# Identity transposes put into the start of a fused attention and two-layer kernel, and a loop step in another order

## The chip, the cores and the metric

The kernel runs on one core of a Trainium2 chip. The metric is device time in microseconds (us), the median of the runs. A core has TensorE (PE in the profile; PEld is its weight load), VectorE (DVE), ScalarE (ACT), GpSimd (POOL) and SyncE (SP, which here only issues DMA transfers). Each engine works through its own instructions strictly in order and waits for others through semaphores. [...]

## The reference

Three parts stand one behind the other. `_attn_ref` is attention in chunks of 32 queries, with 16 positions of left and 8 of right context and 8 memory positions, for 4 batches, 8 heads, 768 positions and 64 values a head. `_moe_ref` and `_moe2_ref` are two dense layers over the 3072 tokens.

```python
# attention, per chunk
scores = scale * np.matmul(q_c, k_full.transpose(0, 1, 3, 2))
a = np.exp(scores - np.max(scores, axis=-1, keepdims=True))
a = a / (np.sum(a, axis=-1, keepdims=True) + 1e-09)
out[:, :, c_start:c_end] = np.matmul(a, v_full)
# first layer, 512 -> 1024 -> 512
h = x @ w_in
e = np.exp(h - h_max)
solu = h * (e / (np.sum(e, axis=-1, keepdims=True) + 1e-09))
ln = (solu - mu) / np.sqrt(var + 1e-06) * g_ln
x = ln @ w_out
# second layer, 512 -> 2048 -> 512
h = x @ w_in2
out = (h * np.clip(h + 3.0, 0.0, 6.0) / 6.0) @ w_out2
```

## The kernel before

The 3072 tokens are cut into 24 tiles of 128. The work on a tile goes through short helper functions, each of which issues a few instructions:

- Attention. `q_p` and `k_p` (from tile 10 on `block_p`, 4 transposes for a whole tile) turn queries and keys on TensorE into one of three PSUM tiles `tp` that go round; `q_e`, `k_e`, `block_e` copy them out. `s_p` makes the scores (16 small products into `sc`, 32 matmul records in the trace), `s_max` and `s_sub` (DVE) take the maximum off, `s_exp` (ACT) exponentiates, `s_sum` (DVE) and `s_norm` (POOL in the loop) normalise, `p_p` transposes the probabilities, `p_e` copies them out, `v_p` makes the value products, and `x_h` (ACT) and `x_l` (DVE) split the result into a high and a low part.
- First layer. `m1(i, f)` is half f of the product with `w_in` (12 matmuls, three for each exact product of split numbers). `ln_max` (DVE), `ln_exp` (ACT), `ln_den`, `ln_solu`, `ln_mean` (DVE), `ln_sq` (ACT), `ln_var` (DVE), `ln_pow` (POOL) and `ln_norm` (DVE) make the normalised activation, `ln_t` transposes it (4 transposes a half, then `ln_h` on ACT and `ln_l` on DVE). `m2` makes the product with `w_out` for three tiles together in pieces of 8 matmuls (`piece`), and `m2_e` (DVE) copies a finished block out.
- Weights arrive as 8-byte numbers and are turned into 4-byte ones by `*_abs`, `*_hold` and `*_bits` (two or three DVE operations each).

The order of the instructions is written out by hand. The list `FIRST` gives it for the start (tiles 0 to 8 in part), name by name. From `m = 7` to 23 a loop gives it: step `m` does `m1` and the normalisation of tile m, attention values of tile `a = m + 1`, scores of tile `n = m + 2`, transposes of tile `l = m - 1`, and up to m = 20 the conversion of two pieces of the second layer's weights (`end_w2`). In a step of even m POOL also adds weight blocks (`sum_pair`). `ln_t(m, 0)`, which needs `ln_norm(m)`, comes in the next step, behind `m1(m + 1, 0)`. The second layer (`g3`, `act3`, `split3`, `g4`) follows the loop.

Of the kernel before, what the change touches and what calls it, by code (L numbers as in the profile page):

```python
# [22 lines left out]

STEADY = 7
FIRST = """
    load_q:0 load_w1:3 q_p:0 load_mem_k:0 mem_p:0 mem_e:0,A zero:km0,D zero:v0,D zero:qb,P q_e:0,0,D w1_abs:3,D
# [4 lines left out]
    mem_e:2,A k_e:1,1,A k_e:1,0,A s_exp:0 s_p:1 w1_abs:0,A w1_abs:2,A k_p:2,0 k_e:2,0,A spread_mem_v:0,0,A zero:v1,P
    w1_hold:7,P w1_bits:7,0 w1_bits:1,1 w1_bits:7,1 w1_bits:1,2 w1_bits:7,2 s_sum:0 w1_hold:0,D w1_bits:0,0
    w1_bits:0,1 w1_hi:3,P s_norm:0,D zero:pb,P p_p:0 q_p:2 load_k:3 load_q:3 load_mem_k:1 load_q:4 load_v:1
    p_e:0,0,A p_e:0,1,A spread_mem_v:0,64,A k_p:2,1 v_p:0 w1_bits:0,2 w1_hi:1,D s_max:1 s_sub:1 s_exp:1 q_e:2,0,D
    x_h:0,0 k_e:2,1,D w1_hi:7,A w1_abs:6,A w1_abs:5,A w1_hold:2,P q_e:2,1,D s_p:2 s_sum:1 w1_bits:2,0 w1_bits:2,1
    s_norm:1,D p_p:1 w1_bits:2,2 p_e:1,0,A w1_abs:4,A p_e:1,1,A w1_hi:2,A w1_lo:1,P w1_lo:3,P s_max:2 w1_hold:5,D
    x_l:0,0 w1_hold:4,D w1_bits:5,0 w1_bits:4,0 w1_bits:5,1 load_k:4 load_wo:4 load_g load_v:2 consts w1_hi:0,P
    w1_lo:0,P w1_hold:6,P w1_lo:7,P w1_lo:2,P load_wo:2 m1:0,0,0 early_open k_p:3,1 k_p:3,0 k_e:3,1,A q_p:3
    k_e:3,0,A q_e:3,1,A q_e:3,0,A w1_bits:4,1 s_sub:2 w1_bits:6,0 w1_bits:5,2 mem_p:1 m1:0,0,1 s_p:3 q_p:4
    w1_bits:6,1 w1_bits:4,2 w1_hi:4,D w1_bits:6,2 w1_lo:4,D w1_hi:5,P spread_mem_v:1,0,A s_exp:2 spread_mem_v:1,64,A  # L40
    v_p:1 w1_hi:6,D s_sum:2 s_max:3 s_norm:2,D s_sub:3 q_e:4,1,A x_h:1,0 q_e:4,0,A mem_e:1,A w1_lo:5,P m1:0,1,0
    w1_lo:6,P k_p:4,1 m1:0,1,1 x_l:1,0 k_e:4,1,D p_p:2 k_p:4,0 m1:1,0,0 s_exp:3 ln_max:0 wo_abs:4,A wo_hold:4,D
    s_sum:3 wo_bits:4,0 s_norm:3,P load_wo:0 load_k:5 load_wo:1 p_e:2,0,A k_e:4,0,A s_p:4 m1:1,0,1 ln_exp:0
    p_e:2,1,A v_p:2 wo_abs:2,A wo_bits:4,1 ln_den:0 s_max:4 ln_solu:0 wo_abs:0,D x_h:2,0 wo_hold:0,D wo_bits:4,2
    s_sub:4 x_l:2,0 ln_mean:0 p_p:3 m1:1,1,0 k_p:5,0 m1:1,1,1 m1:2,0,0 k_p:5,1 m1:2,0,1 s_exp:4 k_e:5,0,A ln_sq:0
    p_e:3,0,A p_e:3,1,A wo_bits:0,0 s_sum:4 wo_g:4 wo_hold:2,P wo_bits:0,1 wo_hi:4,D ln_var:0 k_e:5,1,A wo_abs:1,A
    ln_max:1 wo_bits:0,2 ln_exp:1 wo_bits:2,0 ln_pow:0 wo_hold:1,D wo_bits:2,1 s_norm:4,P ln_norm:0 ln_den:1
    load_q:5 load_v:3 load_k:6 m1:2,1,0 q_p:5 v_p:3 q_e:5,1,A q_e:5,0,A x_h:3,1 p_p:4 p_e:4,0,A load_wo:5 load_q:6
    wo_abs:5,A p_e:4,1,A s_p:5 ln_p:0,0 ln_h:0,0,1 k_p:6,1 m1:2,1,1 k_p:6,0 wo_bits:2,2 wo_g:0 ln_solu:1 ln_mean:1
    wo_bits:1,0 wo_bits:1,1 wo_hi:0,D k_e:6,1,A q_p:6 k_mem:6,D ln_sq:1 load_v:4 load_wo:7 v_p:4 load_w2:0 load_q:7  # L50
    load_wo:3 load_k:7 ln_max:2 wo_g:2 s_edge:5 q_e:6,1,A ln_exp:2 ln_var:1 k_e:6,0,D wo_hi:2,D s_max:5 wo_lo:4,P
    x_l:3,1 wo_lo:0,P m1:3,0,0 x_h:4,1 ln_p:0,1 m1:3,0,1 m1:3,1,0 wo_hold:5,P w2_abs:0,A q_e:6,0,A ln_den:2
    wo_lo:2,D wo_bits:1,2 s_sub:5 s_p:6 q_p:7 k_p:7,0 m1:3,1,1 ln_l:0,0,1 x_l:4,1 ln_pow:1 w2_hold:0,P ln_solu:2
    wo_bits:5,0 m1:4,0,0 wo_abs:7,A s_exp:5 ln_h:0,1,1 wo_hold:7,D wo_g:1 s_sum:5 s_norm:5,P s_edge:6 wo_bits:5,1
    ln_mean:2 w2_bits:0,0 k_e:7,0,A wo_abs:3,A wo_hold:3,P ln_l:0,1,1 ln_sq:2 wo_hi:1,A q_e:7,0,A q_e:7,1,A
    ln_norm:1 ln_p:1,0 m1:4,0,1 k_p:7,1 p_p:5 m1:4,1,0 w2_bits:0,1 ln_max:3 ln_exp:3 ln_h:1,0,1 ln_p:1,1 m1:4,1,1
    k_e:7,1,A wo_bits:5,2 wo_lo:1,P load_v:5 load_wo:6 p_e:5,0,A wo_abs:6,D s_max:6 ln_den:3 ln_var:2 ln_pow:2
    ln_l:1,0,1 s_sub:6 s_exp:6 p_e:5,1,A ln_h:1,1,1 ln_l:1,1,1 ln_norm:2 wo_bits:3,0 ln_solu:3 load_k:8 k_p:8,1
    ln_p:2,0 ln_h:2,0,1 ln_l:2,0,1 s_p:7 k_e:8,1,A load_v:6 load_q:8 v_p:5 early_close k_p:8,0 ln_p:2,1 m2:0,0
    wo_bits:3,1 wo_hold:6,D ln_max:4 ln_exp:4 x_h:5,1 k_e:8,0,A s_sum:6 s_norm:6,P x_l:5,1 p_p:6 q_p:8 wo_bits:6,0  # L60
    ln_den:4 ln_mean:3 ln_solu:4 m1:5,0 s_max:7 wo_g:5 wo_bits:3,2 w2_bits:0,2 wo_g:3 wo_hi:5,P wo_lo:5,P
    wo_bits:6,1 wo_hi:3,D m1:5,1 s_sub:7 ln_mean:4 ln_h:2,1,1 ln_l:2,1,1 q_e:8,1,A ln_sq:3 wo_lo:3,D wo_bits:6,2
    m2:0,1 wo_bits:7,0 ln_var:3 wo_g:6 wo_bits:7,1 wo_bits:7,2 wo_g:7 load_k:9 load_w2:1 w2_store:0 load_w2:2
    w2_abs:1,A p_e:6,0,A p_e:6,1,A v_p:6 q_e:8,0,A w2_hold:1,P ln_pow:3 w2_bits:1,0 ln_norm:3 w2_bits:1,1 wo_hi:6,A
    wo_lo:6,P s_exp:7 s_p:8 w2_abs:2,A wo_hi:7,A wo_lo:7,P m2:0,2 m2:0,3 ln_p:3,0 m2:0,4 ln_p:3,1 x_h:6,1 ln_max:5
    w2_bits:1,2 s_sum:7 x_l:6,1 s_norm:7,D p_p:7 m2:0,5 ln_sq:4 ln_exp:5 ln_h:3,0,1 ln_h:3,1,0 ln_den:5 w2_hold:2,P
    ln_solu:5 m1:6,0 w2_bits:2,0 ln_l:3,0,1 s_max:8 m2_e:0,0 m2:0,6 m2:0,7 m1:6,1 load_v:8 load_w2:3 w2_store:1
    w2_abs:3,A w2_hold:3,P w2_bits:3,0 ln_mean:5 p_e:7,1,A ln_sq:5 w2_bits:2,1 p_e:7,0,D ln_var:5 ln_var:4
    w2_bits:3,1 ln_pow:4 ln_pow:5 w2_bits:3,2 ln_l:3,1,0 ln_norm:4 ln_p:4,1 load_v:7 v_p:7 w2_bits:2,2 ln_max:6
    m2_e:0,1 s_sub:8 ln_norm:5 ln_p:4,0 m2:0,8 m2:0,9 ln_exp:6 ln_h:4,1,0 x_h:7,0 ln_den:6 ln_l:4,1,0 ln_p:5,1  # L70
    m2:0,10 ln_solu:6 x_l:7,0 ln_mean:6 ln_p:5,0 m2:0,11 load_w2:5 w2_store:2 w2_store:3 w2_abs:5,A s_exp:8 s_sum:8
    ln_sq:6 ln_var:6 w2_hold:5,P ln_pow:6 s_norm:8,P ln_norm:6 ln_h:5,1,0 load_w2:4 m2_s:0,1 w2_abs:4,A ln_h:4,0,0
    w2_hold:4,P ln_l:4,0,0 ln_l:5,1,0 ln_h:5,0,0 ln_l:5,0,0 load_q:9 m2_s:0,0 m2_e:0,2 m2_e:0,3 m2_s:0,2 m2_s:0,3
    load_v:9 load_k:10
"""


# [992 lines left out]
```

## Time and profile before

| | |
|---|---|
| median of 3 runs | 955.73 us (955.43 to 956.26) |
| the profiled execution's own time | 956.25 us |
| its span, first to last instruction | 954.2 us |
| TensorE busy | 925.0 us, 97% |
| VectorE busy | 595.9 us, 62% |
| ScalarE busy | 451.0 us, 47% |
| GpSimd busy | 431.5 us, 45% |
| loop (m = 7 to 23) | from 147 us to about 403 us |

A row of a timeline has the start in us, the length in us, the engine, the line of the kernel, the operation, output and input tile, and how many instructions were merged in it; in brackets stands the idle time before it and what ended it. The lengths of neighbouring matmuls overlap, since they are pipelined: what a group costs is the distance between its start and the start of what follows.

### The profile page before, as it was taken

What the parts mean: (1) busy time and instruction counts of PE and PEld (TensorE: products, weight loads), DVE (VectorE), ACT (ScalarE), POOL (GpSimd) and SP (SyncE); (2) the same over time, 40 slices, a digit from 0 to 9 for tenths busy, and PEclk for the clock granted to TensorE, in tenths of its full rate; (3) what the DMA queues carried; (4) which work ended last, traced back from release to release, by engine and by line L of the source; (5) the groups of instructions that cost most, each with busy time, mean ns of one, the idle gap of its engine ahead of it and who ended that gap; (6) DMA issues with size and microseconds to landing.
All of it is one profiled execution on the core that took longest, in us unless ns stands there. A gap on an engine that the chain in (4) does not pass through costs nothing.

```text
span 954.2 us, 20179 instructions
## 1 busy us (share of the span) xinstructions
PE 925.0 (97%) x7740; PEld 867.5 (91%) x7740; DVE 595.9 (62%) x1043; ACT 451.0 (47%) x802; POOL 431.5 (45%) x465
## 2 busy tenths in 40 slices
...
GB/s 178 166 216 183 71 155 169 174 231 199 239 197 232 201 242 133 98 265 233 214 268 86 200 114 164 180 166 154 131 200 78 199 133 164 176 158 170 108 177 100
DMA packets 175626, 165.11 MB, mean 173 GB/s; under 512 B 107436, under 2 KB 128428, under 8 KB 175148
## 3 DMA queue, kind: packets, MB, share of 16 engines
...
q8 instruction: 61, 1.00, 0.4%
q14 instruction: 33, 0.27, 0.1%
...
## 4 chain that ended last, share of the span: by engine, by line
PE 80%; DVE 6%; DMA 5%; issue 3%; POOL 2%; SPq 2%; ACT 1%; DVEq 0%; ACTq 0%; POOLq 0%
PE ph L762 26%; PE acc L816 23%; PE m L607 12%; PE h L522 11%; DMA kn<-in_k_dram 2%; PE tp L491 2%; PE tp L579 2%; PE sc L435 2%; DMA q_raw<-in_q_dram 1%; DMA pair<-w2d 1%; PE tp L473 1%; PE tp L422 1%; SPq L184 1%; DMA b5d<-b_lh 1%; DMA w1raw<-in_moe_w_in_dram 1%
## 5 line engine op out<-in xcount | busy, mean ns | idle before, releaser
L522 PE MATMUL h<-w,xh 128*128 128x512 f32 x336 | 110.4, 410 | 0.2 <-DVE so L548 0.2
L762 PE MATMUL ph<-b_x2r,b_wa 128*128 128x256 f32 x480 | 91.1, 281 | 0.0
L762 PE MATMUL ph<-b_xah,b_wa 128*128 128x256 f32 x480 | 90.7, 280 | 0.0
L777 POOL TENSOR_TENSOR b_pe<-b_pe 128x128 f32<-128x128 f32 x48 | 27.0, 563 | 140.6 <-DVE b_pe L774 140.6
L607 PE MATMUL m<-lnh,wol 128*128 128x384 f32 x256 | 88.8, 347 | 1.6 <-POOL wol L335 0.9
L607 PE MATMUL m<-lnh,woh 128*128 128x384 f32 x256 | 88.4, 345 | 0.8 <-ACT woh L209 0.5
L607 PE MATMUL m<-lnl,woh 128*128 128x384 f32 x256 | 88.4, 345 | 0.0
L777 POOL TENSOR_TENSOR b_pn<-b_pn 128x128 f32<-128x128 f32 x48 | 26.6, 554 | 131.6 <-DVE b_pn L774 130.8
L762 PEld LDWEIGHTS ph<-b_xah,b_wa 128*128 128x128 f32 x480 | 76.1, 188 | 0.0
L762 PEld LDWEIGHTS ph<-b_x2r,b_wa 128*128 128x128 f32 x480 | 76.0, 188 | 0.0
L522 PEld LDWEIGHTS h<-w,xh 128*128 128x128 f32 x336 | 61.0, 192 | 11.9 <-issue 0.3
L237 DVE TENSOR_TENSOR b_ll<-b_xh,b_lh 128x512 fp32r<-128x512 f32 x48 | 33.2, 691 | 58.6 <-ACT b_lh L236 57.3
L222 POOL TENSOR_SCALAR w2t<-w2t 128x512 f32<-128x512 f32 x32 | 62.8, 1970 | 14.2 <-ACT w2t L215 14.1
L522 PE MATMUL h<-w,xl 128*128 128x512 f32 x168 | 67.4, 401 | 1.9 <-DVE xl L252 1.9
L762 PE MATMUL ph<-b_xal,b_wa 128*128 128x256 f32 x240 | 67.4, 281 | 0.0
L567 POOL TENSOR_TENSOR lst<-lst,mhalf 128x1 f32<-128x1 f32 x24 | 15.2, 633 | 115.2 <-DVE lst L562 115.2
L762 PE MATMUL ph<-b_t,b_wa 128*128 128x256 f32 x240 | 67.1, 280 | 0.0
L237 DVE TENSOR_TENSOR b_wb<-b_xh,b_wb 128x512 fp32r<-128x512 f32 x48 | 38.5, 803 | 45.6 <-ACT b_wb L236 45.6
L236 ACT ACTIVATE b_wb<-b_xh 128x512 fp32r<-128x512 f32 x48 | 30.3, 632 | 60.3 <-POOL b_xh L779 60.3
L236 ACT ACTIVATE b_lh<-b_xh 128x512 fp32r<-128x512 f32 x48 | 30.3, 632 | 58.5 <-POOL b_xh L779 58.5
L237 DVE TENSOR_TENSOR b_ll<-b_pe,b_lh 128x384 fp32r<-128x384 f32 x48 | 28.1, 586 | 47.6 <-ACT b_lh L236 47.5
L237 DVE TENSOR_TENSOR b_xal<-b_pn,b_xah 128x384 fp32r<-128x384 f32 x48 | 26.8, 558 | 48.4 <-ACT b_xah L236 48.4
...
## 6 DMA issues: line engine op xcount, KB each, us to landing
...
```

The lines of the kernel that those rows point to most:

```text
L222: ENG[eng].tensor_scalar(out=tf, in0=tf, scalar1=U_LO, scalar2=U_HI, op0=ALU.max, op1=ALU.min)
L236: ACT.activation(out=hi, in_=r, func=AF.Copy)
L237: (eng or DVE).tensor_tensor(lo, r, hi.bitcast(F32), ALU.subtract)
L435: PE.matmul(sc[64 * x:64 * x + 64, c, s], qb[:, p, c].rearrange("k y t -> k (y t)"), kT[i % 2][:, p, c], start=True, stop=True)
L491: PE.matmul(po[64 * x:64 * x + 64, y, :, c * C:(c + 1) * C], vt[:, c, j], pb[:, c, j].rearrange("k s t -> k (s t)"), start=True, stop=True,)
L522: PE.matmul(h[:, f], a[:, kt], w[kt][:, f * 512:(f + 1) * 512], start=n == 0, stop=n == 3 * NKT - 1)
L567: POOL.tensor_tensor(st[:, 10:11], st[:, 9:10], mhalf, ALU.pow)
L579: PE.transpose(pt[:, c], so[:, fc * P:(fc + 1) * P], ident)
L607: PE.matmul(acc, w[fc // 2][:, fc % 2, dc * P:(dc + 1) * P], a[:, fc], start=n == 0, stop=n == len(todo) - 1)
L762: PE.matmul(ph[:, k], w[:, wl, dc * P:(dc + 1) * P], xg[gi][xl][dc], start=m == 0, stop=m == len(todo) - 1)
L777: POOL.tensor_tensor(q[:, 6], q[:, 0], q[:, 3], ALU.add)
L816: PE.matmul(out, a[al][:, blk], w[:, wl], start=j == 0 and m == 0 and PLACE[p][1] == 0, stop=j == NS - 1 and m == 2, skip_group_check=True)
```

## The change

The list `FIRST` gets twelve entries `warm:n`, 83 in sum, and is otherwise the same. `warm(n)` issues n transposes of the identity matrix into a PSUM tile of its own that nobody reads; the tile's pool is closed where `early_open` opens another. In the loop the order of the helpers changes: `q_p`, `q_e` stand behind `block_p`, `block_e` and ahead of `ln_exp`; `v_p` and `s_p` stand side by side behind `piece(m, 2)`, with `x_h`, `x_l` behind them; `s_max` and `s_sub` stand ahead of `ln_var`, and `s_exp` follows `ln_norm`.

```diff
-    load_q:0 load_w1:3 q_p:0 load_mem_k:0 mem_p:0 mem_e:0,A zero:km0,D zero:v0,D zero:qb,P q_e:0,0,D w1_abs:3,D
+    load_q:0 load_w1:3 warm:10 q_p:0 warm:14 load_mem_k:0 mem_p:0 warm:6 mem_e:0,A zero:km0,D zero:v0,D zero:qb,P
...
-        pools = {}
+        pools = {"w": ExitStack()}
+        idle = pools["w"].enter_context(tc.tile_pool(name="idle", bufs=1, space=PSUM))
+
+        def warm(n):
+            t = idle.tile([P, 4, P], F32, tag="w", name="idle")
+            for j in range(n):
+                PE.transpose(t[:, j % 4], ident, ident)
+
         def early_open():
+            pools["w"].close()
...
+            if ok(n) and n >= BLOCKS:
+                q_p(n)
+                q_e(n, 0, "A")
+                q_e(n, 1, "A")
             ln_exp(m)
             if w2u:
                 end_w2(w2u[1])
             piece(m, 1)
-            if ok(n) and n >= BLOCKS:
+            if n < BLOCKS:
+                k_p(n, 1)
+                k_e(n, 1, "A")
                 q_p(n)
                 q_e(n, 0, "A")
                 q_e(n, 1, "A")
-            if ok(a):
-                v_p(a)
             ln_den(m)
             ln_solu(m)
             ln_mean(m)
...
+            piece(m, 2)
+            if ok(a):
+                v_p(a)
+            if ok(n):
+                s_p(n)
+                if n % TPB in (0, TPB - 1):
+                    s_edge(n)
             if ok(a):
                 x_h(a)
                 x_l(a)
-            if n < BLOCKS:
-                k_p(n, 1)
-                k_e(n, 1, "A")
-            if n < BLOCKS:
-                q_p(n)
-                q_e(n, 0, "A")
-                q_e(n, 1, "A")
-            piece(m, 2)
             ln_sq(m)
+            if ok(n):
+                s_max(n)
+                s_sub(n)
             ln_var(m)
             ln_pow(m)
...
             piece(m, 3)
             ln_norm(m)
             if ok(n):
-                s_p(n)
-                if n % TPB in (0, TPB - 1):
-                    s_edge(n)
+                s_exp(n)
...
-            if ok(n):
-                s_max(n)
-                s_sub(n)
-                s_exp(n)
```

How this moves instructions shows at three places. TensorE in a loop step, before: the value products (L491) stand behind the query transposes (L422), and the scores (L435) stand 17 rows below, ahead of the next `m1`.

```order
L607 MATMUL m_2892<-lnh,wol 128x384
L607 MATMUL m_2892<-lnh,woh 128x384
L422 MATMUL tp<-ident,q_raw 128x128 x4
L491 MATMUL tp<-pb,v_88 64x2x32 x16
L607 MATMUL m_2892<-lnl,woh 128x384
L607 MATMUL m_2892<-lnh,wol 128x384
```

TensorE in a loop step, now (the query transposes stand 16 rows above, right behind those of the keys):

```order
L607 MATMUL m_3240<-lnh,woh 128x384
L607 MATMUL m_3240<-lnl,woh 128x384
L491 MATMUL tp<-pb,v_89 64x2x32 x16
L435 MATMUL sc<-kT,qb 64x64 x16
L607 MATMUL m_3240<-lnh,wol 128x384
L607 MATMUL m_3240<-lnh,woh 128x384
```

So between full-size matmuls there is now one stretch of small products in a step, where there were two.

VectorE in a loop step, before, from the copy of a finished block (L612) over `ln_den` (L542, L543), `ln_solu` (L548), `ln_mean` (L553), `x_l` (L252), `ln_var` (L562) and `ln_norm` (L572) to `s_max` (L447) and `s_sub` (L452):

```order
L612 COPY x2o<-m_3578 128x384
L542 TENSOR_SCALAR lst<-lst 128x1
L543 RECIPROCAL lst<-lst 128x1
L548 SCALAR_TENSOR_TENSOR so,lst<-h,lst,e 128x1024
L553 TENSOR_SCALAR lst<-lst 128x1
L252 TENSOR_TENSOR xl<-tp,xh 128x512
L562 TENSOR_SCALAR lst<-lst 128x1
L572 TENSOR_SCALAR so<-so,lst 128x1024
L447 TENSOR_REDUCE ast<-sc 128x8
L452 TENSOR_TENSOR pe<-sc,ast 128x512
```

VectorE, the same step, now:

```order
L612 COPY x2o<-m_3699 128x384
L542 TENSOR_SCALAR lst<-lst 128x1
L543 RECIPROCAL lst<-lst 128x1
L548 SCALAR_TENSOR_TENSOR so,lst<-h,lst,e 128x1024
L553 TENSOR_SCALAR lst<-lst 128x1
L252 TENSOR_TENSOR xl<-tp,xh 128x512
L447 TENSOR_REDUCE ast<-sc 128x8
L452 TENSOR_TENSOR pe<-sc,ast 128x512
L562 TENSOR_SCALAR lst<-lst 128x1
L572 TENSOR_SCALAR so<-so,lst 128x1024
```

L447 and L452 have moved ahead of L562 and L572. ScalarE in a loop step, as a difference, from the last key copy to `ln_sq` (L557):

```order
 L209 ACTIVATE kT<-tp 128x4x24
-L537 ACTIVATE e,lst<-h,lst 128x1024
-L209 ACTIVATE qb<-tp 64x16x32 x2
+L209 ACTIVATE qb<-tp 64x16x32 x2
+L537 ACTIVATE e,lst<-h,lst 128x1024
 L248 ACTIVATE xh<-tp 128x512
 L557 ACTIVATE e,lst<-so,lst 128x1024
```

`ln_exp` (L537) now stands behind the two copies of `q_e`.

## Rows read from the trace of the kernel before

**Rows 1.** Windows of TensorE: stretch, length, busy (instructions), granted clock, DMA share, GB/s.
```profile
123.00:402.00 279.00, 277.86 (x2365) 1.00 0.70 190
```

**Rows 2.** Timeline of TensorE, one loop step: value products and scores stand apart.
```profile
269.02 1.15 PE L491 MATMUL tp<-pb,v 128*64 128x64 f32 x32
270.10 0.44 PE L607 MATMUL m<-lnh,woh 128*128 128x384 f32 x1
270.39 0.34 PE L607 MATMUL m<-lnl,woh 128*128 128x384 f32 x1
...
272.81 0.34 PE L607 MATMUL m<-lnh,woh 128*128 128x384 f32 x1
273.08 1.15 PE L435 MATMUL sc<-kT,qb 128*64 128x64 f32 x32
274.17 0.73 PE L522 MATMUL h<-w,xh 128*128 128x512 f32 x2
```

**Rows 3.** Timeline of TensorE ahead of the loop: both stand together.
```profile
114.26 1.15 PE L491 MATMUL tp<-pb,v 128*64 128x64 f32 x32
115.24 1.10 PE L435 MATMUL sc<-kT,qb 128*64 128x64 f32 x32
116.27 0.45 PE L607 MATMUL m<-lnl,woh 128*128 128x384 f32 x1
```

**Rows 4.** Timeline of TensorE: `ln_t` around the steps m = 14, 15 and 18.
```profile
264.40 0.60 PE L579 MATMUL tp<-ident,so 128*128 128x128 f32 x4
...
277.07 0.63 PE L579 MATMUL tp<-ident,so 128*128 128x128 f32 x4
...
280.30 0.60 PE L579 MATMUL tp<-ident,so 128*128 128x128 f32 x4
...
327.99 0.60 PE L579 MATMUL tp<-ident,so 128*128 128x128 f32 x4
```

**Rows 5.** Timeline of VectorE, step m = 14, from `ln_den` to `s_sub`.
```profile
271.77 0.14 DVE L542 TENSOR_SCALAR lst<-lst 128x1 f32<-128x1 f32 x1
...
273.54 0.68 DVE L252 TENSOR_TENSOR xl<-tp,xh 128x512 fp32r<-128x512 f32 x1
274.99 0.15 DVE L562 TENSOR_SCALAR lst<-lst 128x1 f32<-128x1 f32 x1 [0.77 <-ACT e L557]
275.82 1.10 DVE L572 TENSOR_SCALAR so<-so,lst 128x1024 f32<-128x1024 f32 x1 [0.68 <-POOL lst L567]
276.84 0.68 DVE L447 TENSOR_REDUCE ast<-sc 128x8 f32<-128x512 f32 x1
277.56 0.69 DVE L452 TENSOR_TENSOR pe<-sc,ast 128x512 f32<-128x512 f32 x1
```

**Rows 6.** Timeline of VectorE: `ln_norm` in the step m = 18.
```profile
339.02 1.10 DVE L572 TENSOR_SCALAR so<-so,lst 128x1024 f32<-128x1024 f32 x1 [0.20 <-POOL lst L567]
```

**Rows 7.** Timeline of ScalarE, step m = 15: `ln_exp`, then `q_e`.
```profile
284.91 1.13 ACT L537 ACTIVATE e<-h,lst 128x1024 f32<-128x1024 f32 x1
286.00 1.21 ACT L209 ACTIVATE qb<-tp 64x512 f32<-64x512 f32 x2
```

**Rows 8.** Timeline of TensorE in the start: four query transposes, and what follows them.
```profile
26.81 1.09 PE L422 MATMUL tp<-ident,q_raw 128*128 128x128 f32 x4 [0.76 <-DMA q_raw<-in_q_dram]
27.69 0.42 PE L393 MATMUL tp<-ident,kn 128*128 128x128 f32 x1
...
42.54 1.11 PE L422 MATMUL tp<-ident,q_raw 128*128 128x128 f32 x4
...
48.70 0.66 PE L422 MATMUL tp<-ident,q_raw 128*128 128x128 f32 x4
```

**Rows 9.** Windows of TensorE, from the first query transposes to the first `m1`.
```profile
5.74:35.12 29.38, 20.88 (x180) 1.00 1.05 180
```

**Rows 10.** Timeline of VectorE: its waits for TensorE between 38 and 55 us.
```profile
52.76 0.62 DVE L211 COPY kT<-tp 128x448 f32<-128x448 f32 x1 [0.61 <-PE tp L394]
...
54.37 1.23 DVE L531 TENSOR_REDUCE lst<-h 128x1 f32<-128x1024 f32 x1 [0.98 <-PE h L522]
```

More of the change, by code (lines that the diff above doesn't have):

```diff
@@ L31 @@
[L31 to L74, printed above, removed]
+    load_q:0 load_w1:3 warm:10 q_p:0 warm:14 load_mem_k:0 mem_p:0 warm:6 mem_e:0,A zero:km0,D zero:v0,D zero:qb,P
+    q_e:0,0,D w1_abs:3,D zero:kn0,P zero:kn1,D load_k:0 k_p:0,1 load_w1:7 load_mem_k:2 load_mem_k:3 load_w1:1
@@ new lines @@
+    load_q:1 w1_hold:3,P q_e:0,1,D k_p:0,0 warm:6 k_e:0,0,D k_mem:0,D mem_p:3 k_e:0,1,A s_p:0 warm:5 w1_abs:1,A
+    w1_abs:7,A q_p:1 warm:8 q_e:1,1,A q_e:1,0,A zero:km1,D load_k:1 load_w1:0 load_k:2 load_w1:2 load_q:2 load_v:0
+    load_w1:6 load_w1:5 load_w1:4 w1_bits:3,0 w1_bits:3,1 w1_hold:1,D mem_e:3,D w1_bits:3,2 s_edge:0 k_p:1,1 mem_p:2
+    k_p:1,0 warm:6 s_max:0 w1_bits:1,0 s_sub:0 mem_e:2,A k_e:1,1,A k_e:1,0,A s_exp:0 s_p:1 warm:4 w1_abs:0,A
+    w1_abs:2,A k_p:2,0 warm:6 k_e:2,0,A spread_mem_v:0,0,A zero:v1,P w1_hold:7,P w1_bits:7,0 w1_bits:1,1 w1_bits:7,1
@@ new lines @@
+    w1_bits:1,2 w1_bits:7,2 s_sum:0 w1_hold:0,D w1_bits:0,0 w1_bits:0,1 w1_hi:3,P s_norm:0,D zero:pb,P p_p:0 warm:6
+    q_p:2 load_k:3 load_q:3 load_mem_k:1 load_q:4 load_v:1 p_e:0,0,A p_e:0,1,A spread_mem_v:0,64,A k_p:2,1 v_p:0
+    w1_bits:0,2 w1_hi:1,D s_max:1 s_sub:1 s_exp:1 q_e:2,0,D x_h:0,0 k_e:2,1,D w1_hi:7,A w1_abs:6,A w1_abs:5,A
+    w1_hold:2,P q_e:2,1,D s_p:2 warm:8 s_sum:1 w1_bits:2,0 w1_bits:2,1 s_norm:1,D p_p:1 warm:4 w1_bits:2,2 p_e:1,0,A
+    w1_abs:4,A p_e:1,1,A w1_hi:2,A w1_lo:1,P w1_lo:3,P s_max:2 w1_hold:5,D x_l:0,0 w1_hold:4,D w1_bits:5,0
@@ new lines @@
+    w1_bits:4,0 w1_bits:5,1 load_k:4 load_wo:4 load_g load_v:2 consts w1_hi:0,P w1_lo:0,P w1_hold:6,P w1_lo:7,P
+    w1_lo:2,P load_wo:2 m1:0,0,0 early_open k_p:3,1 k_p:3,0 k_e:3,1,A q_p:3 k_e:3,0,A q_e:3,1,A q_e:3,0,A
+    w1_bits:4,1 s_sub:2 w1_bits:6,0 w1_bits:5,2 mem_p:1 m1:0,0,1 s_p:3 q_p:4 w1_bits:6,1 w1_bits:4,2 w1_hi:4,D
+    w1_bits:6,2 w1_lo:4,D w1_hi:5,P spread_mem_v:1,0,A s_exp:2 spread_mem_v:1,64,A v_p:1 w1_hi:6,D s_sum:2 s_max:3
+    s_norm:2,D s_sub:3 q_e:4,1,A x_h:1,0 q_e:4,0,A mem_e:1,A w1_lo:5,P m1:0,1,0 w1_lo:6,P k_p:4,1 m1:0,1,1 x_l:1,0
@@ new lines @@
+    k_e:4,1,D p_p:2 k_p:4,0 m1:1,0,0 s_exp:3 ln_max:0 wo_abs:4,A wo_hold:4,D s_sum:3 wo_bits:4,0 s_norm:3,P
+    load_wo:0 load_k:5 load_wo:1 p_e:2,0,A k_e:4,0,A s_p:4 m1:1,0,1 ln_exp:0 p_e:2,1,A v_p:2 wo_abs:2,A wo_bits:4,1
+    ln_den:0 s_max:4 ln_solu:0 wo_abs:0,D x_h:2,0 wo_hold:0,D wo_bits:4,2 s_sub:4 x_l:2,0 ln_mean:0 p_p:3 m1:1,1,0
+    k_p:5,0 m1:1,1,1 m1:2,0,0 k_p:5,1 m1:2,0,1 s_exp:4 k_e:5,0,A ln_sq:0 p_e:3,0,A p_e:3,1,A wo_bits:0,0 s_sum:4
+    wo_g:4 wo_hold:2,P wo_bits:0,1 wo_hi:4,D ln_var:0 k_e:5,1,A wo_abs:1,A ln_max:1 wo_bits:0,2 ln_exp:1 wo_bits:2,0
```

31 lines of the change are left out of this document (27 added, 4 removed).

## The prediction, made before the changed kernel was run

> **What bounds the kernel now.** I read the busy shares first, then the waits of TensorE, then the timelines of the stages that the change touches. From 123 to 402 us, the end of the start and the whole loop, TensorE is busy 277.86 of 279 us [rows 1]: a loop step lasts as long as TensorE's own instructions, and the reader is to see that no other engine's time counts there as long as it comes in time. How much time it has left is read from one place. A step needs its `ln_norm` for the first `ln_t` transposes, which stand in the next step. Count from the second `ln_t` of step 14, at 264.40: `ln_norm` starts at 275.82 and lasts 1.10, to 276.92 [rows 5], and the transposes that need it start at 277.07 [rows 4], 0.15 later. There is no slack at all: VectorE is as late as TensorE. In step 18 `ln_norm` starts at 339.02 [rows 6], 11.03 after 327.99 [rows 4], against 11.42 in step 14: 0.39 to spare. So the loop stands on two legs, TensorE's sum and the chain `ln_max`, `ln_exp`, `ln_solu`, `ln_sq`, `ln_norm`.
>
> In the start TensorE is busy 20.88 of 29.38 us between the first query transposes and the first `m1`, and waits the other 8.5 [rows 9]. Its level there can't be read from the column of the granted clock, which says 1.00 [rows 9]: four query transposes at 42.54 last 1.11, and four at 48.70 last 0.66 [rows 8], so I read the level as the low one (1.2 GHz) until about 48 us and the high one (2.4 GHz) after.
>
> **The change part by part: the order on TensorE.** Before a group of 64-wide products there is a longer gap, and behind it too: 272.81 to 273.08 is 0.27, 270.10 to 270.39 is 0.29 [rows 2], where a matmul of that size follows the next every 0.17 ((272.81 - 270.39) / 14). So `v_p` and `s_p` apart cost 2 x (0.10 + 0.12) in borders and 1.08 + 1.09 for themselves [rows 2], 2.61. Together they take 0.98 + 1.03 [rows 3] and one entry and exit, 2.23. TensorE saves 0.38 a step, 15 steps (m = 7 to 21) have both, so 5.7 us if nothing else ends last. The transposes that now stand together cost what they did: no border is seen in the rows around them, and I book nothing for them.
>
> **The order on VectorE.** `ln_var` comes behind `s_max` and `s_sub`. In step 14 `x_l` starts at 273.54 and takes 0.68, `s_max` 0.72 to the next start, `s_sub` 0.69 [rows 5], so `ln_var` can start at 275.63, not 274.99: 0.64 later. Before, VectorE waited 0.77 for `ln_sq` there, and that idle time covers the rest of the 1.41. From `ln_var` to `ln_norm` it stays 0.83 (274.99 to 275.82, through POOL), then 1.10 and 0.15. The transposes come at 277.71, 13.31 after 264.40; from there to the next second `ln_t` it is 3.23 (277.07 to 280.30 [rows 4]); the step takes 16.54 instead of 15.90. In step 14 nothing hides it, in step 18 0.39 are free. I take +0.40 for an even step, from +0.25 (step 18) and +0.64.
>
> **The order on ScalarE.** `ln_exp` waits behind two `q_e` copies. That hurts where VectorE was earlier than in step 14, as in step 15: the copies take 1.21, so `ln_exp` goes from 284.91 to 286.12 and ends at 287.25 [rows 7]. Then `ln_den` to `x_l` 1.77 (271.77 to 273.54 [rows 5]), x_l, s_max, s_sub 2.09, 0.83, 1.10, 0.15: the transposes at 293.2, 12.9 after 280.30 [rows 4], plus 3.23 is 16.1 against some 15.9 before. I take +0.25 for an odd step, between 0 (a step with slack as step 18) and +0.5 (a step where the block copy of `m2_e`, moved with its piece, stands ahead of `x_l`).
>
> The pattern holds in 13 steps (m = 8 to 20, with `end_w2`): 7 x 0.40 + 6 x 0.25 = 4.3. Step 7 (keys still in the longer form of `k_p`, so longer on TensorE) and step 21 (no `end_w2`) have time to spare and give 0.38 each back. Sum of the loop +3.5 us, with bounds from -5.7 (TensorE alone) to 7 x 0.64 + 6 x 0.5 - 0.8 = +6.7. `load_q`, `load_k`, `load_v` and the stores stand behind the same waits of SyncE as before; `x_l` is due only with the third matmul of the next `m1` and comes earlier than `ln_norm`, so it is next in line but not the end.
>
> **The fills.** 83 transposes of the identity. At the low level four take 0.88 (26.81 to 27.69 [rows 8]), 0.22 each; at the high level I take half, 0.11. The first ten run ahead of the first data. The other 73 are 16.1 us at the low level, into waits of 8.5 [rows 9]: TensorE would come to the first `m1` up to 7.6 late. At the high level they are 8.0, they fit, and all other work of TensorE there is halved. What that is worth is little: between 38 and 55 us, where TensorE passes from the low to the high level, VectorE has two waits for it, 0.61 and 0.98 [rows 10]. A faster TensorE pulls VectorE, which converts the weights all the while, by at most 1.6 us. I take -1.0, since the first microseconds still run at the low level and delay the copies behind them.
>
> If the level doesn't rise, part of the 7.6 goes into waits of TensorE that the first `m1` has anyway for the split weights; I take +4.0, between +1 and +6. Does it rise? The four transposes at 42.54, behind eight of keys, still ran at the low level, and those at 48.70, behind `m1` products and scores, no longer did [rows 8]. Half of the key transposes are small (24 rows of keys), with less work in a microsecond than the fills, so the trace doesn't decide. The Trainium skill, "TensorE: Matmul & The Clock Gate", section "Part 4: PE-mode transpose", says that the full rate does not engage for transposes; by it the fills would run at 0.22 throughout and the sum would take +4.0 instead of -1.0. The rows at 42.54 and 48.70 agree with it as far as they go.
>
> **Sum.** Loop +3.5, start -1.0: +2.5. The profiled execution took 956.25 (span 954.2), 0.5 above the median of 955.73; against the median the forecast is 958.2.
>
> **The rivals.**
> 1. *The fills stay at the low level.* For it: the low level through 42.54 [rows 8]. Against: denser fills. Loop +3.5, start +4.0: 963.2.
> 2. *Faster: the chain to `ln_norm` isn't the end.* If `ln_norm` starts within 11.0 us of the second `ln_t` in all steps (12.67 less 0.38 less 1.10 less 0.15), TensorE's sum decides. For it: step 18 is there now, and steps that last longer give SyncE's loads and ScalarE time, so that VectorE starts its part earlier. Against: the step 14, and that the delays follow from order alone. Loop -5.7, start -1.0: 949.0. With fills at the low level 954.0.
> 3. *It does about nothing:* the gains of the steps with slack pay for the steps without, start as before: 955.7.
>
> **How the numbers follow.** Forecast 0.40 (958.2, its own range 956 to 961), rival 1 0.25, rival 2 0.15 and its low-level variant 0.08, rival 3 0.12. Below 951 lies some 0.1 (rival 2), above 963.5 as much (rival 1), so the range is 951 to 963.5. Differences under 0.2%, 1.9 us, can't be told from none: faster means below 953.8, slower above 957.6. Slower: 0.6 of the forecast and nearly all of rival 1, 0.48. Faster: rival 2 and half its variant and a little of the rest, 0.25. Same: 0.27.
>
> **What would show it.** Right: in steps 8 to 20 TensorE waits for DVE L572 ahead of `ln_t` by 0.5 to 1 us, steps last 16.1 to 16.5, `v_p` and `s_p` together take about 2.0; `ln_exp` starts 1.2 later behind `p_p`. In the start four query transposes last 0.6 to 0.66 well before 40 us (forecast) or 1.1 (rival 1). Wrong: no wait at L579 in the loop and steps of 15.5; or `ln_t` waits, but steps under 15.9.

## The result, and the profile after

The changed kernel takes 960.92 us (median of 4 runs, 960.38 to 963.72), the kernel before 955.8 on the same chip: ratio 1.0061, with a 95% interval of 1.0039 to 1.0083. The profiled execution took 961.46 us (span 959.4), 5.21 more than that of before (956.25). Count the loop from the second `ln_t` of step 7 to that of step 23: 149.75 to 405.44 before, 149.28 to 410.71 now. The start gave 0.47, the loop took 5.74, and what follows the loop is unchanged. A step is counted below from its second `ln_t` to that of the next step.

First the waits of TensorE for `ln_norm` (total, times, longest, in us), before:

```profile
PE tp L579 <- DVE so L572: 1.4, 2, 1.2
PE tp L579 <- DVE sc L441: 0.7, 1, 0.7
```

and after:

```profile
PE tp L579 <- DVE so L572: 9.5, 14, 1.2
```

The window of TensorE after that answers to [rows 1], with the same columns:

```profile
123.00:402.00 279.00, 270.20 (x2311) 1.00 0.68 188
```

TensorE, which had been busy for all but 1.1 of these 279 us, now is idle for 8.8, and nearly all of it (8.36) in one place: 13 waits ahead of the first `ln_t`. (The 14th, 1.17 at 89.52, stands ahead of the loop, and was there before.) The next fence shows TensorE in step 14 (answers to [rows 3] and [rows 4]):

```profile
266.03 0.60 PE L579 MATMUL tp<-ident,so 128*128 128x128 f32 x4
...
272.07 1.15 PE L491 MATMUL tp<-pb,v 128*64 128x64 f32 x32
273.05 1.10 PE L435 MATMUL sc<-kT,qb 128*64 128x64 f32 x32
274.08 0.44 PE L607 MATMUL m<-lnh,wol 128*128 128x384 f32 x1
...
279.38 0.63 PE L579 MATMUL tp<-ident,so 128*128 128x128 f32 x4 [0.74 <-DVE so L572]
...
282.62 0.60 PE L579 MATMUL tp<-ident,so 128*128 128x128 f32 x4
```

Value products and scores together take 2.01, as they did ahead of the loop. The transposes come 13.35 behind the second `ln_t` (12.67 before), and the step lasts 16.59 (15.90 before). VectorE in the same step (answers to [rows 5]):

```profile
273.55 0.14 DVE L542 TENSOR_SCALAR lst<-lst 128x1 f32<-128x1 f32 x1
...
275.33 0.68 DVE L252 TENSOR_TENSOR xl<-tp,xh 128x512 fp32r<-128x512 f32 x1
275.93 0.68 DVE L447 TENSOR_REDUCE ast<-sc 128x8 f32<-128x512 f32 x1
276.71 0.69 DVE L452 TENSOR_TENSOR pe<-sc,ast 128x512 f32<-128x512 f32 x1
277.32 0.15 DVE L562 TENSOR_SCALAR lst<-lst 128x1 f32<-128x1 f32 x1
278.14 1.10 DVE L572 TENSOR_SCALAR so<-so,lst 128x1024 f32<-128x1024 f32 x1 [0.68 <-POOL lst L567]
```

`s_max` and `s_sub` stand where VectorE used to wait 0.77 for `ln_sq`, and push `ln_var` from 10.59 to 11.29 behind the second `ln_t`. On ScalarE in step 15 `ln_exp` follows the two copies of `q_e` and starts 5.83 behind the second `ln_t` at 282.62, against 4.61 (answers to [rows 7]):

```profile
287.23 1.20 ACT L209 ACTIVATE qb<-tp 64x512 f32<-64x512 f32 x2
288.45 1.11 ACT L537 ACTIVATE e<-h,lst 128x1024 f32<-128x1024 f32 x1
```

The start, TensorE (answers to [rows 8]):

```profile
4.38 1.12 PE L422 MATMUL tp<-ident,q_raw 128*128 128x128 f32 x4 [0.64 <-DMA q_raw<-in_q_dram]
5.28 2.64 PE L862 MATMUL idle<-ident 128*128 128x128 f32 x14
...
16.33 0.66 PE L422 MATMUL tp<-ident,q_raw 128*128 128x128 f32 x4 [1.39 <-DMA q_raw<-in_q_dram]
...
20.67 1.39 PE L862 MATMUL idle<-ident 128*128 128x128 f32 x6
...
25.35 0.88 PE L862 MATMUL idle<-ident 128*128 128x128 f32 x6
26.07 0.60 PE L473 MATMUL tp<-ident,pn 128*128 128x128 f32 x4
...
38.87 0.50 PE L522 MATMUL h<-w,xl 128*128 128x512 f32 x1 [1.97 <-DVE xl L252]
...
42.00 1.11 PE L422 MATMUL tp<-ident,q_raw 128*128 128x128 f32 x4
...
48.29 0.66 PE L422 MATMUL tp<-ident,q_raw 128*128 128x128 f32 x4
```

The same four transposes take 1.12 at 4 us, 0.66 at 16 us, 1.11 at 42 us and 0.66 at 48 us. So the level was the high one (2.4 GHz) by 16 us, where it had still been the low one (1.2 GHz) at 42 before, and it did not stay there. It rose among the 14 fills that start at 5.28: from start to start they take 0.21 up to 7.20 and 0.11 behind it. The column of the granted clock (busy, granted clock, DMA share, GB/s) shows the falls:

```profile
15.00:20.00 5.00, 2.86 (x21) 1.00 1.10 192
20.00:25.00 5.00, 5.00 (x49) 0.66 1.11 169
...
30.00:35.00 5.00, 4.46 (x65) 0.66 0.98 250
35.00:40.00 5.00, 2.66 (x14) 1.00 1.22 206
40.00:45.00 5.00, 4.99 (x20) 0.63 0.76 123
```

The first and the third fall come behind a stretch in which TensorE was busy 2.86 and 2.66 of 5 us. VectorE had waited 0.61 and 0.98 in [rows 10]; now there is no idle time ahead of either, but its `ln_max` starts only 0.43 earlier (53.94 against 54.37). The waits went away in the main because VectorE comes later: it had waited for ScalarE (1.25 and 0.94 at 38 and 40 us, against 0.44 in one wait), and the `s_max` ahead of them starts at 50.77, against 49.59.

### The profile page after: what moved, and what is told of

It reads as the page before. It is cut to its first block, busy times and chain, and to the rows that moved or that the text cites. A ratio compares the mean times of both kernels' runs of the same rounds, so it can differ in the third digit from the quotient of the medians.

```text
span 959.4 us, 20328 instructions
## 1 busy us (share of the span) xinstructions
PE 928.5 (97%) x7823; PEld 872.0 (91%) x7823; DVE 595.0 (62%) x1043; ACT 451.8 (47%) x802; POOL 430.5 (45%) x465
## 4 chain that ended last, share of the span: by engine, by line
PE 67%; issue 10%; DMA 9%; DVE 7%; POOL 5%; ACT 2%; SPq 1%; DVEq 0%; ACTq 0%; POOLq 0%
PE ph L762 25%; PE acc L816 23%; PE m L607 7%; PE h L522 6%; DMA w2raw<-in_moe_w_out_dram 3%; DMA kn<-in_k_dram 2%; PE tp L579 1%; POOL w2t L222 1%; PE tp L491 1%; DMA q_raw<-in_q_dram 1%; DMA b2d<-b_km 1%; DMA pair<-w2d 1%; DVE so L572 1%; DMA v<-in_v_dram 1%; DMA w1raw<-in_moe_w_in_dram 1%
## 5 line engine op out<-in xcount | busy, mean ns | idle before, releaser
L522 PE MATMUL h<-w,xh 128*128 128x512 f32 x336 | 107.9, 402 | 0.0
```

Source lines behind the costliest of these rows:

```text
L522: PE.matmul(h[:, f], a[:, kt], w[kt][:, f * 512:(f + 1) * 512], start=n == 0, stop=n == 3 * NKT - 1)
```

## The experiments

All are timed against the kernel before, on the chip on which they ran (955.3 to 955.5 us there).

**The fills alone.** Only the list `FIRST`, `warm` and the pool of its tile are changed; the loop is that of before.

> The kernel before with the 83 fills alone, the loop untouched. Theory (the loop's order costs the time, the fills give 0.5 us): 955.3 us, within 1 us of before, the loop's first step begins some 0.5 us earlier, steps of 15.9 us. Rival (the fills cost time, since the level falls again three times and the loads are disturbed): 957 to 961 us. Second rival (the fills alone are worth the full 1.6 us of VectorE's two waits): 954.1 us.

954.52 us (12 runs), ratio 0.9985 (0.9973 to 0.9998). Loop 255.25, as before. The fills bring a little under 1 us: step 7 begins at 147.60 in this profile, and in the nine other kernels here with fills between 145.6 and 149.6, against 149.75, 149.09 and 148.38 in those without. The start itself varies by more than the fills bring. The spread goes roughly with the level. Up to step 7 all ten kernels with fills hold the same instructions, and in each the fills come down to 0.11 between 5 and 12 us. But in the kernel with `v_p` and `s_p` apart (below) the level never falls in the start, and step 7 begins at 145.59; TensorE there:

```profile
38.63 0.66 PE L422 MATMUL tp<-ident,q_raw 128*128 128x128 f32 x4
```

These are the transposes that take 1.11 at 42.00 in the changed kernel. In the two other kernels that have them at 0.66 step 7 begins at 146.93 and 147.60, in the seven that do not at 147.85 to 149.56. Each is one profile, so that the falls take most of the gain back is argued, not shown.

**The loop order alone.** The fills are left out.

> The changed kernel without the fills; the loop in the new order. Theory: the loop from the second ln_t of step 7 to that of step 23 takes 261.4 us as in the changed kernel (255.7 before), so 961.5 us. Rival (the fills make the loss): 956 us or less.

966.21 us (6 runs), ratio 1.0099 (1.0076 to 1.0122). Slower than the whole change, which my theory did not expect. Loop 266.41, waits at L579 11.2 us. Its costliest step, 10, lasts 19.45: `ln_norm` comes late, and then this (TensorE, windows of 2 us):

```profile
212.00:214.00 2.00, 0.33 (x2) 1.00 1.14 325
214.00:216.00 2.00, 1.74 (x8) 0.76 0.61 126
216.00:218.00 2.00, 2.00 (x6) 0.50 0.41 91
```

Behind a wait of 1.93 the level fell to the low one (0.50, 1.2 GHz) for some 3 us, and from the first `ln_t` to the second it takes 4.80 instead of 3.23.

**`ln_exp` put back.**

```diff
+            ln_exp(m)
             if ok(n) and n >= BLOCKS:
                 q_p(n)
                 q_e(n, 0, "A")
                 q_e(n, 1, "A")
-            ln_exp(m)
```

> The changed kernel, with ln_exp ahead of the two query copies again; s_max and s_sub stay ahead of ln_var. Theory (two delays add up on the chain to ln_norm; this one decides where VectorE is early, in steps of odd m and those with slack): ln_den at 5.9 to 6.4 instead of 7.06 after the second ln_t in odd steps, the wait ahead of ln_t goes there from 0.5-0.75 to about 0, even steps keep 16.2 to 17.1 us; 958 us. A new wait of 0.1 to 0.3 us at the scores for the later query copies is possible. Rival (the new order of TensorE itself costs the time): no change, 961 us.

955.05 us (12 runs), ratio 0.9995 (0.9976 to 1.0014); loop 255.42. That is 3 below what was expected, and the rival is out. Odd steps last 15.5 without a wait. Six of the seven even steps with `end_w2` still wait 0.44 to 1.28. In step 14 the reason is seen on VectorE, in the two halves of W2:

```profile
263.49 0.42 DVE L226 TENSOR_SCALAR w2t<-w2t 128x512 uint32<-128x512 uint32 x1
263.94 0.69 DVE L229 SCALAR_TENSOR_TENSOR w2t<-w2raw,w2t 128x512 uint32<-128x512 uint32 x1
...
265.28 1.52 DVE L226 TENSOR_SCALAR w2t<-w2t 128x512 uint32<-128x512 uint32 x1
266.83 1.11 DVE L229 SCALAR_TENSOR_TENSOR w2t<-w2raw,w2t 128x512 uint32<-128x512 uint32 x1
267.98 1.10 DVE L232 SCALAR_TENSOR_TENSOR w2t<-w2raw,w2t 128x512 uint32<-128x512 uint32 x1
269.47 0.14 DVE L542 TENSOR_SCALAR lst<-lst 128x1 f32<-128x1 f32 x1
```

The same operation takes 0.42 and 1.52. The second stands beside GpSimd's pair sum (264.95 to 269.67): the six operations of the two halves take 5.53 there and 3.60 in step 15, without it. The Trainium skill, "GPSIMD Engine Reference", section "8. Key points", says that GpSimd shares its SBUF interfaces with VectorE and that they contend where VectorE has two SBUF inputs or runs in a 2-port mode. The two-input rows agree (0.69 becomes 1.11 and 1.10); the operation with one tensor input suffers too, and in which mode it runs no row here shows.

**`s_max` and `s_sub` put back behind `ln_norm`.**

```diff
             ln_sq(m)
-            if ok(n):
-                s_max(n)
-                s_sub(n)
             ln_var(m)
...
             ln_norm(m)
             if ok(n):
+                s_max(n)
+                s_sub(n)
                 s_exp(n)
```

> The changed kernel, with s_max and s_sub behind ln_norm again; ln_exp stays behind the query copies. Theory: ln_norm comes 0.5 to 0.65 us earlier in all steps, odd steps 15.5 to 15.7 us, even steps some 15.9 to 16.3; the loop 7 us shorter than in the changed kernel, 954 us, below before by 1 to 2. Rival (VectorE's order is covered, ScalarE's alone makes the loss): 960 us or more.

953.36 us (12 runs), ratio 0.9976 (0.9962 to 0.999); loop 253.78. This edit alone takes back 7.65 of the loop's 261.43. Odd steps last 15.5 to 15.7 without a wait; the largest wait left (1.07, step 16) is behind `ln_pow`, which stands behind a late pair sum on GpSimd.

**The whole chain put first.** `ln_exp` moves right behind the second `ln_t`; `ln_den`, `ln_solu`, `ln_mean` and `ln_sq` ahead of the second half of W2; `ln_var`, `ln_pow`, `x_h`, `x_l` and `ln_norm` ahead of `s_edge`, `s_max` and `s_sub`.

```diff
             ln_t(l, 1)
+            ln_exp(m)
...
-            ln_exp(m)
-            if w2u:
-                end_w2(w2u[1])
+            ln_den(m)
+            ln_solu(m)
+            ln_mean(m)
...
+            ln_sq(m)
+            if w2u:
+                end_w2(w2u[1])
...
                 s_p(n)
-                if n % TPB in (0, TPB - 1):
-                    s_edge(n)
+            ln_var(m)
+            ln_pow(m)
             if ok(a):
                 x_h(a)
                 x_l(a)
-            ln_sq(m)
+            ln_norm(m)
...
```

> The changed kernel with its new order on TensorE, but with the chain to ln_norm put first wherever it shares a queue: ln_exp right behind the second ln_t on ScalarE, then ln_den, ln_solu and ln_mean ahead of the halves of W2 on VectorE, ln_sq ahead of x_h, and ln_var, ln_pow, x_l and ln_norm ahead of s_max and s_sub. My theory (the loop's loss is the wait of the next step's first ln_t for ln_norm, 9.5 us on TensorE of the changed kernel, because exp, ln_den and ln_var come 1.2 us later in a step than before): the wait goes to under 1 us in sum, a step takes what TensorE's own instructions take, 15.5 us odd and even, the loop from step 7 to step 23 takes 248 to 251 us against 261.4, and the whole some 949 to 951 us. Rival, that TensorE itself lost time by the new order (scores beside value products, transposes together): steps stay at 15.9 to 16.1, about 256 us of loop and 956 in all. Rival, that something else ends late once the chain is early (the exponentials of the scores or x_l, which now wait for ln_norm): the wait moves to h or to p_p, about 2 to 4 us of it in sum, 952 to 955.

956.48 us (12 runs), ratio 1.001 (0.9997 to 1.0023); loop 254.65. A miss: the expectation was 949 to 951. The chain starts 3 us earlier (`ln_exp` 1.46 to 2.42 behind the second `ln_t`, about 4.6 before), `ln_norm` stands at 8.5 to 10.6 except in 10 and 16, and yet no step up to 21 is under 15.48: that is TensorE's own sum. In the steps 10 and 16 TensorE waits 1.66 and 2.00 for `ln_norm`, more than in the changed kernel (0.88 and 1.14). GpSimd and VectorE in step 16:

```profile
303.76 1.29 POOL L678 TENSOR_TENSOR sums<-pair 128x512 f32<-128x512 f32 x1 [8.18 <-DMA pair<-w2d]
...
307.09 0.56 POOL L567 TENSOR_TENSOR lst<-lst,mhalf 128x1 f32<-128x1 f32 x1
...
307.69 0.81 DVE L572 TENSOR_SCALAR so<-so,lst 128x1024 f32<-128x1024 f32 x1 [4.52 <-POOL lst L567]
```

The pair sum waits 8.18 for its load, `ln_pow` stands behind it, and `ln_norm` behind that. An earlier chain can't pass it. The sum itself starts later than in the changed kernel, 8.92 and 9.56 behind the second `ln_t` of the two steps against 8.42 and 8.67. And what was pushed back (`s_max` and all behind it, to the probabilities that the next step needs) has moved behind that late `ln_norm`; what that costs was not measured apart.

**`v_p` and `s_p` apart again.**

```diff
-            piece(m, 2)
             if ok(a):
                 v_p(a)
+            piece(m, 2)
             if ok(n):
                 s_p(n)
```

> The changed kernel, but v_p stands ahead of the third piece of the wide products, so that value products and scores are 4.4 us apart again as they were before the change, and all else is as changed. My theory (VectorE's chain to ln_norm sets the step, not TensorE's own sum): x_h comes earlier on VectorE but the chain stays as late, so the loop stays at 259 to 263 us and the whole at 959 to 963. Rival, that bringing the two together saved TensorE the 0.4 to 0.5 us in each step that the rows of before show for it (0.64 against 0.98 us): the loop loses 16 times 0.35 = 5.6 us, and the whole is at 966 to 968.

961.19 us (6 runs), ratio 1.0066 (1.0048 to 1.0083); loop 263.46. The total is that of the change, as expected; in its profile the loop is 2.0 longer and step 7 began earlier (145.59). TensorE in step 12 is back to two stretches of 1.08:

```profile
234.19 1.15 PE L491 MATMUL tp<-pb,v 128*64 128x64 f32 x32
235.27 0.44 PE L607 MATMUL m<-lnh,wol 128*128 128x384 f32 x1
...
236.86 1.15 PE L435 MATMUL sc<-kT,qb 128*64 128x64 f32 x32
237.94 0.44 PE L607 MATMUL m<-lnl,woh 128*128 128x384 f32 x1
```

The step lasts 16.16, as in the changed kernel, and of its wait of 0.47 only 0.12 is left. The steps 9, 12, 13 and 19 are the same to 0.02; steps 7 and 21, which TensorE decides, are 0.36 longer each, and the rest of the 2.0 is in the even steps 14, 18 and 20 (+1.7), with the pair sum beside the conversions, less what 8 and 11 gain (0.5). So in the changed kernel the saving of 0.36 to 0.38 a step is there and is turned into waiting.

**Both chain edits together.** `ln_exp` ahead of `q_e` and `s_max`, `s_sub` behind `ln_norm`.

> The changed kernel with two of its lines put back: ln_exp ahead of the two copies of q_e on ScalarE, and s_max and s_sub behind ln_norm on VectorE (each alone gave 955.1 and 953.4 us). My theory: the two have one and the same wait to take away, so they do not add up. Odd steps are at 15.5 in both already; in even steps the wait that is left (0.6 to 1.3 us) comes from the halves of W2 on VectorE beside the pair sum on GpSimd, and the later copies of q_e cost a small wait at s_p. Loop 251 to 254 us, whole 951 to 954. Rival, that they add up in full (6 and 7.6 us): 947 to 948.

952.08 us (12 runs), ratio 0.9957 (0.9941 to 0.9974): faster than both kernels. Loop 252.60; as expected the edits don't add up. Steps 11 to 15 and 17 to 19 take 15.49 to 15.53, the step of before less 0.36. TensorE in step 14, where nothing waits any more:

```profile
262.64 0.60 PE L579 MATMUL tp<-ident,so 128*128 128x128 f32 x4
...
274.94 0.60 PE L579 MATMUL tp<-ident,so 128*128 128x128 f32 x4
```

Its waits for `ln_norm` in the whole span:

```profile
PE tp L579 <- DVE so L572: 3.2, 4, 1.2
```

One of the four, 1.16, stands ahead of the loop. What is left are mainly the steps 8, 10 and 16 (17.52, 16.34 and 16.84). All even steps hold a pair sum; in 10 and 16 its load lands late, and `ln_pow` starts only behind it (11.27 and 11.77 behind the second `ln_t`, 9.57 to 11.00 in 12, 14, 18 and 20).

**Both, and the pair sum one step later.** In the odd step behind `s_norm`, with its store.

```diff
-            if m % 2 == 0:
-                sum_pair(m // 2 - 4)
+            if m % 2 and m > 8 and m < NTILE - 1 or m == NTILE - 2:
+                sum_pair((m - m % 2) // 2 - 4)
...
```

> The kernel with both chain edits (ln_exp ahead of q_e, s_max and s_sub behind ln_norm; 952.1 us), and beside it GpSimd's pair sum one step later: in the odd step behind s_norm, where its operands have landed long before, instead of at the head of the even step, where it waits for its load. My theory (what is left of the wait for ln_norm comes from the pair sum, in steps 10 and 16 because it keeps ln_pow waiting on GpSimd, in the others because VectorE's W2 conversions beside it take 5 to 6 us instead of 3.6): steps 10 and 16 go from 16.34 and 16.84 to 15.5 or 15.6, odd steps now have the slower conversions but room for them (ln_den at 7 instead of 5.9, due at 7.3) and stay within 0.3 of 15.5; loop 250 to 251.5 us against 252.6, whole 950 to 951. Rival, that the conversions beside the pair sum cost an odd step as much as they cost the even one: loop 252 to 254, whole 952 to 953.

955.25 us (12 runs), ratio 0.9993 (0.998 to 1.0006); loop 255.63. The theory was half right: the steps 8, 10 and 16 go to 16.57, 15.50 and 15.49. But 11 and 17 take 18.30 and 18.72, and 15 takes 16.47. GpSimd and TensorE in step 17:

```profile
308.70 3.81 POOL L222 TENSOR_SCALAR w2t<-w2t 128x512 f32<-128x512 f32 x2 [4.04 <-ACT w2t L215]
312.48 1.04 POOL L465 TENSOR_TENSOR pn<-pe,ast 128x512 f32<-128x512 f32 x1
...
313.58 0.66 PE L473 MATMUL tp<-ident,pn 128*128 128x128 f32 x4 [1.58 <-POOL pn L465]
```

The W2 pieces of step 16 land late, `w2_hold` waits for them on GpSimd, `s_norm` stands behind it, and `p_p` waits.

**The change with the pair sum one step later.** The same edit on the changed kernel.

> The changed kernel with only GpSimd's pair sum moved from the even to the odd step. My theory: even and odd steps change places. The next step's first ln_t starts 12.9 us behind the second one in an even step (13.7 now in most) and 13.4 to 13.9 in an odd step (12.9 now), the wait at ln_t moves with it, and the loop stays at 259 to 262 us, the whole at 959 to 962. Rival, that the pair sum has nothing to do with it and even steps are longer for their own work (another block copy, the stores): even steps stay at 13.7.

960.75 us (6 runs), ratio 1.0051 (1.0036 to 1.0066); loop 262.68. Counted from the second `ln_t` to the next first one, even steps went to 12.9 (14; 12 and 18 stood there) and 13.2 (10, 16), as the theory has it; odd ones stayed at 13.0 to 13.4, so the places did not change, but for 11 and 17 (15.29 and 15.16, late W2 pieces again). In an odd step of the changed kernel the conversions end before `ln_exp` does, so their slowing is hidden.

**The loop order without fills, with the pair sum one step later.**

> The changed kernel without the fills, and with GpSimd's pair sum moved to the odd step. The loop order without fills took 966.2 us, 5 more than with them, though the fills alone are worth about 1. My theory: the other 4 us came from where the pair loads happened to land (in step 10 ln_norm 1.3 us later than in the changed kernel, a wait of 3.2 us on TensorE and a fall of the granted clock to 0.50 behind it). With the pair sum out of its load's way the kernel is within 0.5 to 2 us of the same one with fills, 960 to 963. Rival, that the loop order needs the fills (its TensorE comes out of the start at the low level otherwise, or too late): still some 5 us more, 965 to 967.

962.0 us (6 runs), ratio 1.0066 (1.0049 to 1.0083): 1.25 more than the same kernel with fills. The fills are worth about 1 us with this loop too, though the runs of the two overlap (960.46 to 965.28, and 959.61 to 961.87). The other 4 of the loop order alone went away with the pair sum, so they came from where in a step it runs. In step 10 it had run 1.05 later than in the changed kernel (its load was issued 4.86 behind the second `ln_t`, against 3.95) and kept `ln_pow` waiting. In 12, 14, 18 and 20 it had run 0.7 to 2.3 earlier, beside more of the conversions: `ln_den` started 0.4 to 1.0 later, and these steps were longer by 0.43 to 0.96, 2.8 together. Why its time differs stays open.

**The store of the sums back at the even step.**

```diff
-            if m % 2 and m > 8 and m < NTILE - 1 or m == NTILE - 2:
-                SP.dma_start(out=b5f[(m - m % 2) // 2 - 4], in_=raw["sums"])
+            if m % 2 == 0 and m > 8 and m < NTILE - 2:
+                SP.dma_start(out=b5f[m // 2 - 5], in_=raw["sums"])
+            if m >= NTILE - 3 and m < NTILE - 1:
+                SP.dma_start(out=b5f[m // 2 - 4], in_=raw["sums"])
```

> The kernel with both chain edits and the pair sum in the odd step (955.3 us), with one thing put back: the store of the sums (640 KB) stands at the end of an even step again, behind the loads of the tile, and not at the end of the odd step ahead of the pair load. My theory: in the kernel before this one all steps from 9 on lasted 15.5 us but for 11 and 17 (18.3 and 18.7) and 15 (16.5), because the store ran in steps 10 and 16 beside the W2 loads, these came late, and behind them on GpSimd w2_hold and s_norm, for which p_p waited. With the store out of there these steps go to 15.5 to 16.3, the loop from 255.6 to 249 to 251 us, and the whole to 948.5 to 951, at or below the best so far (952.1). Rival, that the W2 loads of steps 10 and 16 are late by themselves (the value loads with the memory rows stand in the same queue there): these two steps stay above 17, the loop at 253 to 255, and nothing is won over 952.

953.17 us (12 runs), ratio 0.9978 (0.9966 to 0.999); loop 255.62 in a profile of 955.8. The theory is out, and the rival is nearer: nothing is won over 952, and step 11 is down only to 17.11, with W2 late by itself. But what neither had is step 17 (19.69): the store now holds the one buffer of the sums, and the pair sum waits for it with `ln_pow` behind:

```profile
319.40 1.30 POOL L678 TENSOR_TENSOR sums<-pair 128x512 f32<-128x512 f32 x1 [8.29 <-DMA b5f<-sums]
...
322.74 0.56 POOL L567 TENSOR_TENSOR lst<-lst,mhalf 128x1 f32<-128x1 f32 x1
```

It is no better than both chain edits alone, 952.08. A second buffer for the sums was not tried.

## Why the prediction was right

The forecast was 958.2, the result 960.92: +5.1 on the same chip, where I had +2.5. Direction and mechanism hold in the loop, and it is mis-sized; in the start the size is about right, and the mechanism is not.

**TensorE's saving: right.** Together the two take 2.01, and with the chain out of the way a step lasts 15.50 against 15.86 to 15.88: 0.36 to 0.38, as worked out. In the changed kernel it becomes waiting: with the two apart again the total is the same, and steps that `ln_norm` ends keep their length. "No slack at all" was too much, though. It held in step 14, but not in the odd steps. In step 15 of the kernel before, `ln_norm` was over at 291.54, 1.42 ahead of the transposes (0.15 in step 14):

```profile
290.44 1.10 DVE L572 TENSOR_SCALAR so<-so,lst 128x1024 f32<-128x1024 f32 x1 [0.20 <-POOL lst L567]
292.96 0.60 PE L579 MATMUL tp<-ident,so 128*128 128x128 f32 x4
```

So, less that 0.15, 0.9 to 1.5 were free in the six odd steps from 9 to 19.

**VectorE's order: right.** In step 14 I had +0.64, and it is +0.69. Of the two chain edits it is the larger: putting it back alone gives 7.65 us of loop, putting `ln_exp` back alone 6.01, and both together only 8.83, since the same wait goes away.

**ScalarE's order: mis-sized.** `ln_exp` starts 1.22 later, as worked out from the two copies (1.21). The step worked through, 15, came out right (transposes 12.98 behind the second `ln_t`, I had 12.9; +0.34). But I averaged it with steps that keep time to spare and took +0.25. None kept any: `ln_den` waits for `ln_exp` in all six odd steps (9 to 19), as here in step 15, and starts at 7.06 to 7.08 in each (5.85 to 6.43 before), so that `ln_norm` comes 1.2 to 2.2 later and takes all that was free.

```profile
289.69 0.15 DVE L542 TENSOR_SCALAR lst<-lst 128x1 f32<-128x1 f32 x1 [1.01 <-ACT e L537]
```

These steps lost 0.30 to 0.77, 0.47 in the mean. Four lost 0.30 to 0.34; 13 and 19, where the block copy of `m2_e` stands ahead of `x_l`, lost 0.75 and 0.77, and I had +0.5 for such a step. That is 6 x 0.22 = 1.3 of the error.

**Even steps: +0.52 in the mean instead of +0.40**, 0.84 over seven. Step 16 alone lost 1.12: GpSimd's pair sum, which I had left out of the chain, ends behind `ln_var` there and delays `ln_pow`. Step 10 lost only 0.11, because the sum had been late there before, too (16.73, against 15.87 with the fills alone). **Steps 7 and 21** gave 0.32 and 0.37 (I had 0.38). The two errors are the 2.2 by which the loop is over my +3.5.

**The fills: the size right in part by luck, -1.0 against -0.5 in this profile, -0.8 in the fills alone and -1.25 with the loop order.** Rival 1 is out: the level rose while almost nothing but transposes of the identity had run, and six fills that took 0.22 each at the low level take 0.12 at 25 to 27 us. The Trainium skill's rule for the transpose mode ("TensorE: Matmul & The Clock Gate", "Part 4: PE-mode transpose"), weighed in the prediction, does not hold here; by it these would have stayed at 0.22. Read as in the prediction, it does not fit the row at 48.70 either: four transposes took 0.66 there without any fill. That the level falls again I had not expected. My price was VectorE's two waits. They went away, 1.59 us, but only 0.43 of it reached `ln_max`, since VectorE came 1.18 later to them. Whether 1.6 is the most that a faster TensorE can give stays open: where the level did not fall, step 7 began 4.2 earlier than before (145.59 against 149.75), in one profile. And the high level halves the fills, but not "all other work": four query transposes go from 1.11 to 0.66.

**The rivals.** Rival 2 (TensorE's sum decides) is out for this kernel, and it is what the kernel with both chain edits comes near: 952.1, where I had 949.0. Rival 3 (about nothing) is out: the interval of the ratio begins at 1.0039.
